# The last 64 keys of each head over 128 rows, and the causal masks at the end of their score banks

## The chip, the cores and the metric

The kernel runs on one core of a Trainium2 chip. What counts is the device time of one execution in microseconds, here the median of several runs. TensorE (PE) multiplies and writes PSUM banks. ScalarE (ACT), VectorE (DVE) and GpSimd (POOL) work on PSUM and SBUF. SyncE (SP) issues all DMAs of this kernel. PEld in the profile is TensorE's weight load, which can run beside a matmul.

## The reference

Attention over 4 x 8 heads with 576 positions of width 64, then two feed-forward blocks over the 2304 resulting rows. Cut to what matters:

```python
scores = scale * np.matmul(q, k.transpose(0, 1, 3, 2))
causal = np.triu(np.ones((S, S), dtype=bool), k=1)
cum = np.cumsum(np.maximum(s, 0.0), axis=-1)
bias = -(cum[:, :, :, None] - cum[:, :, None, :])
scores = np.where(causal, -1000000000.0, scores + np.minimum(bias, 0.0))
attn = softmax(scores)                     # max subtracted, sum + 1e-9
x = np.matmul(attn, v)                     # 32 heads, 576 x 64 each
h = x @ moe_w_in;   x = (h - np.tanh(h)) @ moe_w_out        # 512 -> 2048 -> 512
h = x @ moe2_w_in;  g = h * np.clip(h + 3, 0, 6) / 6;  out = g @ moe2_w_out
```

## The kernel before

**Stages.** PE first works through the 32 heads (until 208 us), then through the first feed-forward block (lines 831 and 862, until about 599 us), then through the second one, done with seven products instead of eight (lines 1123 and 1199, to the end). ACT, DVE and POOL prepare operands beside it, and in the attention they also turn the feed-forward weights, which come as 64-bit numbers, into pairs of high and low 32-bit parts (lines 753 to 780).

**A head.** Scores are computed transposed: keys on the 128 PSUM partitions, queries along the free dimension. 576 keys are four tiles of 128 and one tile of 64 (`j` = 4). For each head:

- Line 481 (`mx`) multiplies queries with keys for the row maxima; line 490 on DVE (`rd`, tile `junk`) reduces them into `Mt`; lines 515 to 519 bring them into the layout `mrow`, and two DMAs write them out and into the rows of `Q1` (`mdram<-mrow`, `Q<-mdram`).
- Line 575 (`st`) fills four score banks, 0 to 3. `CHUNKS` says which tile of keys `j` and which queries lie in a bank; `STEPS` gives the order of its matmuls. A step `h` multiplies the tiles `K2` and `Q2` over 128 rows, a step `l` the tiles `K1` and `Q1` over 68 rows (two of them carry the cumulative sum, two the maximum), and the number behind the letter is the place in `CHUNKS`. The step `m` adds the causal mask: it multiplies the bf16 identity `identb` with columns of `maskT`, 128, 192 or 256 of them (banks 0, 2 and 3; bank 1 has none). The first step of a bank carries `start`, the last one `stop`.
- Line 578 on ACT (`ex`) takes the exponential of a bank into a tile `pt`.
- Line 606 (`pv`) multiplies V (`vf`, 66 columns: 64 of V, then ones for the row sums) with `pt` and sums into two banks. These operands are 32-bit floats in full precision, and the trace has two matmul records for each such multiplication, two passes. In bank 2 the first product belongs to the last 64 keys (`j` = 4): 64 rows, 64 columns.
- Line 629 on ACT (`ov`) copies the sums out, and line 636 stores the row of sums.

**What sets the order.** All instructions of all engines stand in an order that a planner works out ahead (`Plan.schedule`, with the priorities of `PRIO` and costs by the number of columns). Neither costs nor priorities depend on the order of `STEPS` or on the number of rows, so that the order around the change stays. In PE's order the four banks of one head's scores stand between the sums (line 606) and the maxima (line 481) of its neighbours.

**Tables that the change touches.** The values of V arrive as 640 rows, of which the last 64 are zeros (`values` in `_layout`). In bank 2 the 64 keys fill partitions 0 to 63 of the first 64 columns; on partitions 64 to 127 of these columns only the mask is written, and it is -8e9 there, so that `pt` is 0.

Of the kernel before, what the change touches and what calls it, by code (L numbers as in the profile page):

```python
# [19 lines left out]
B, H, S, D = 4, 8, 576, 64  # L20
NT, DM, DFF = B * S, H * D, 2048
P = 128
# [3 lines left out]
DV = D + 2  # L26
# [18 lines left out]

MASKS = [(1, 64, 128), None, (1, 0, 192), (2, 64, 128)]

STEPS = ["h0 m l0", "h0 l0", "h1 h0 l0 m l1", "h1 h0 m l1 l0"]

MAXT = [[(2, 384, 0), (4, 576, 384)], [(3, 512, 0)], [(1, 256, 0), (0, 128, 256)]]  # L50
TINY, HUGE = (float(np.array([b], np.uint32).view(np.float32)[0]) for b in (0x38000000, 0x47F00000))
# [177 lines left out]
def mm_us(n, f32=False):  # L229

    return (4 * n / 2.4 + 6) / 1e3 if f32 else max(0.1, (n / 2.4 + (13 if n > 128 else 5)) / 1e3)


def vec_us(n, ghz, fixed):
    return (n / ghz + fixed) / 1e3
# [3 lines left out]
def kernel(  # L239
# [55 lines left out]
    def r(b):  # L295
        return late[b.t] if isinstance(b.t, str) else b.t
# [260 lines left out]
    def scores(h, hh, t0, b1, b2, vf, deps, lv, xp, xb, bt, sds):  # L557
        def st(c, b):
            qa, ka, qb, kb = (t[:, hh] for t in r(b1) + r(b2))
            ps = r(b)  # L560
            segs = CHUNKS[c]

            def step(x):
                if x == "m":
                    k, m0, n = MASKS[c]
                    o = ps[:, 0 : k * 192].rearrange("p (k n) -> p k n", k=k)[:, :, 0:n]
                    return o, identb, maskT[:, m0 : m0 + k * n].rearrange("p (k n) -> p k n", k=k)
                kk, qq, n_r = (kb, qb, P) if x[0] == "h" else (ka, qa, 68)
                j, q0, n, col = segs[int(x[1])]
                rr = min(P, S - j * P)  # L570
                return ps[0:rr, col : col + n], kk[0:n_r, j * P : j * P + rr], qq[0:n_r, q0 : q0 + n]

            mms = [step(x) for x in STEPS[c].split()]
            for i, (o, w, x) in enumerate(mms):
                nc.tensor.matmul(o, w, x, start=(i == 0), stop=(i == len(mms) - 1), skip_group_check=True)  # L575

        def ex(c, b, pt):
            nc.scalar.activation(r(pt), r(b)[:, 0 : CW[c]], AF.Exp, scale=0.125)  # L578

        exs, pts, sts = [], [], []  # L580
        for c in range(4):
            b, pt = Buf(banks), Buf(ptp[c])
            us = sum(2 * mm_us(n) for _, _, n, _ in CHUNKS[c]) + (mm_us(MASKS[c][0] * MASKS[c][2]) if MASKS[c] else 0)
            so = plan.op("PE", us, lambda c=c, b=b: st(c, b), deps, [b1, b2, b], t0 + PRIO["st"] + PRIO["dst"] * c, name=f"st{h}_{c}")
            sts.append(so)
            exs.append(plan.op("ACT", vec_us(CW[c], 1.2, 165), lambda c=c, b=b, pt=pt: ex(c, b, pt), [so], [b, pt], t0 + PRIO["ex"] + PRIO["dst"] * c, name=f"ex{h}_{c}"))
            pts.append(pt)
        st_done[h] = sts
        po = [Buf(banks, greedy=True) for _ in range(2)]

        def segments(c):
            segs = []
            for j, q0, n, col in CHUNKS[c]:
                if q0 < 256:
                    n0 = min(256 - q0, n)
                    segs.append((j, 0, q0, n0, col))
                    if n > n0:
                        segs.append((j, 1, 0, n - n0, col + n0))
                else:
                    segs.append((j, 1, q0 - 256, n, col))  # L600
            return segs

        def pv(c):
            for j, bank, oc, n, col in segments(c):
                rr = min(P, S - j * P)
                nc.tensor.matmul(  # L606
                    r(po[bank])[0:DV, oc : oc + n], r(vf)[0:rr, j, hh, :], r(pts[c])[0:rr, col : col + n],
                    start=(j == 0), stop=(bank == 0 and c == 2) or (bank == 1 and j == 2),
                )

        pvs = []
        for c in range(4):
            us = sum(mm_us(n, True) for _, _, _, n, _ in segments(c))
            used = sorted({x[1] for x in segments(c)})
            pvs.append(plan.op(
                "PE", us, lambda c=c: pv(c), [exs[c], lv] + pvs[-1:],
                [vf, pts[c]] + [po[i] for i in used], t0 + PRIO["pv"] + PRIO["dst"] * c, name=f"pv{h}_{c}",
            ))
        pv_done.extend(pvs)

        sg = Buf(stagep) if hh else None
        own = [sg] if hh else [xb]

        def ov(bank):
            q0, n = ((0, 256), (256, 320))[bank]
            dst = r(sg) if hh else xp()
            nc.scalar.activation(dst[0:DV, q0 : q0 + n], r(po[bank])[0:DV, 0:n], AF.Copy)

        ov0 = plan.op("ACT", 0.36, lambda: ov(0), [pvs[2]], [po[0]] + own, t0 + PRIO["ov"], name=f"ov{h}_0")
        ov1 = plan.op("ACT", 0.42, lambda: ov(1), [pvs[3], ov0], [po[1]] + own, t0 + PRIO["ov"], name=f"ov{h}_1")

        def sd_():
            src = r(sg) if hh else xp()
            nc.sync.dma_start(sdram[bt, h % H : h % H + 1, :], src[D : D + 1, :])

        sd = plan.dma(sd_, 2, [ov1], own, t0 + PRIO["sd"], name=f"sd{h}")
        batch_sd.setdefault(bt, []).append(sd)
        if hh:  # L640
            so = plan.dma(lambda: nc.sync.dma_start(xp()[64:128], r(sg)[0:D, :]), 147, [sds[0], ov1], own + [xb], t0 + PRIO["so"], name=f"so{h}")
            batch_so.setdefault(bt, []).append(so)
        return sd
# [678 lines left out]
```

## Time and profile before

| what | value |
|---|---|
| median of 3 runs | 967.13 us (966.61 to 970.09) |
| the profiled execution | 967.26 us, of which the span of its instructions 965.5 us |
| PE busy | 943.3 us, 98% of the span |
| DVE, ACT, POOL busy | 671.8, 467.6, 160.8 us |
| granted clock of PE | 1.00 |

The profile's page gives for each engine how long it was busy, and the chain of work that ended last: from the last instruction back to whatever released each one. The windows view gives busy time by stretch; the timeline gives the instructions in order of time, with runs of the same line merged to one row. A matmul's start in the trace is when it enters the engine, and its end is modelled, so that neighbours overlap; distances from one start to a later start are what can be added up.

### The profile page before, as it was taken

What the parts mean: (1) busy time and instruction counts of PE and PEld (TensorE: products, weight loads), DVE (VectorE), ACT (ScalarE), POOL (GpSimd) and SP (SyncE); (2) the same over time, 40 slices, a digit from 0 to 9 for tenths busy, and PEclk for the clock granted to TensorE, in tenths of its full rate; (3) what the DMA queues carried; (4) which work ended last, traced back from release to release, by engine and by line L of the source; (5) the groups of instructions that cost most, each with busy time, mean ns of one, the idle gap of its engine ahead of it and who ended that gap; (6) DMA issues with size and microseconds to landing.
All of it is one profiled execution on the core that took longest, in us unless ns stands there. A gap on an engine that the chain in (4) does not pass through costs nothing.

```text
span 965.5 us, 14956 instructions
## 1 busy us (share of the span) xinstructions
PE 943.3 (98%) x5560; PEld 833.1 (86%) x5560; DVE 671.8 (70%) x1107; ACT 467.6 (48%) x714; POOL 160.8 (17%) x106
## 2 busy tenths in 40 slices
PE   3999999999999999999999999999999999999998
PEld 3777777778878888998888888999999999999998
DVE  7887767769998667767766834556775567764763
ACT  2677677755444443543443433444454434544442
POOL 8344656520000000003223222000000000000000
PEclk9999999999999999999999999999999999999999
DMA  4767777677535357556455690776797767977663
GB/s 123 183 165 177 212 189 202 161 253 255 172 115 189 141 209 239 174 183 224 158 214 170 221 319 30 249 218 211 237 321 229 226 208 238 319 223 228 207 220 104
DMA packets 70521, 195.91 MB, mean 203 GB/s; under 512 B 11634, under 2 KB 20338, under 8 KB 69168
## 3 DMA queue, kind: packets, MB, share of 16 engines
q1 hardware_dynamic: 70448, 194.95, 63.5%
q8 instruction: 44, 0.72, 0.3%
q14 instruction: 29, 0.24, 0.1%
HBM read 143.75 MB, written 44.09 MB: 195 GB/s over the span
## 4 chain that ended last, share of the span: by engine, by line
PE 93%; DVE 3%; DMA 2%; ACT 1%; issue 1%; SPq 0%; DVEq 0%; ACTq 0%
PE bank L831 20%; PE bank L862 20%; PE pair L1199 19%; PE pair L1123 18%; PE bank L606 9%; PE bank L575 5%; PE wide L481 1%; DVE junk L490 1%; PE bank L481 1%; DMA Q<-Q 1%; DMA Q<-mdram 0%; ACT w L779 0%; DVE K L430 0%; DVE f_w L1143 0%; DMA K<-rb 0%
## 5 line engine op out<-in xcount | busy, mean ns | idle before, releaser
L862 PE MATMUL bank<-gg,w 128*128 128x512 f32 (+1 forms) x960 | 234.3, 368 | 0.5 <-ACT gg L850 0.3
L831 PE MATMUL bank<-xx,w 128*128 128x512 f32 (+1 forms) x960 | 233.3, 368 | 0.0
L862 PEld LDWEIGHTS bank<-gg,w 128*128 128x128 f32 x960 | 170.1, 189 | 30.9 <-ACT gg L850 1.3
L831 PEld LDWEIGHTS bank<-xx,w 128*128 128x128 f32 x960 | 170.5, 188 | 30.3
L1123 PE MATMUL pair<-op_w,w 128*128 128x384 f32 x648 | 118.0, 334 | 0.6 <-DVE f_w L1143 0.6
L842 ACT ACTIVATE g<-bank 128x512 f32<-128x512 f32 (+1 forms) x80 | 44.5, 556 | 147.6 <-PE bank L831 124.3
L1199 PE MATMUL pair<-w,op_W 128*128 128x256 f32 x918 | 115.1, 283 | 0.0
L1123 PEld LDWEIGHTS pair<-op_w,w 128*128 128x128 f32 x648 | 112.4, 188 | 1.2 <-DVE f_w L1143 0.9
L1199 PEld LDWEIGHTS pair<-w,op_W 128*128 128x128 f32 x918 | 112.8, 192 | 0.0
L606 PE MATMUL bank<-pt,vf 128*66 128x320 f32 (+4 forms) x448 | 112.3, 364 | 0.3 <-ACT pt L578 0.3
L852 POOL TENSOR_TENSOR gg<-g,gg 128x512 fp32r<-128x512 f32 x32 | 47.5, 1485 | 345.0 <-ACT gg L850 307.9
L575 PE MATMUL bank<-Q,K 128*128 128x320 f32 (+9 forms) x384 | 98.0, 368 | 1.6 <-DMA Q<-mdram 1.2
L846 DVE TENSOR_TENSOR g<-bank,g 128x512 f32<-128x512 f32 (+1 forms) x80 | 50.9, 636 | 64.8 <-ACT g L842 64.1
L578 ACT ACTIVATE pt<-bank 128x512 f32<-128x512 f32 (+2 forms) x128 | 63.1, 501 | 40.9 <-PE bank L575 36.4
L575 PEld LDWEIGHTS bank<-Q,K 128*128 128x128 f32 (+3 forms) x384 | 64.8, 188 | 20.7 <-DMA Q<-mdram 1.3
L850 ACT ACTIVATE gg<-g 128x512 fp32r<-128x512 f32 (+1 forms) x80 | 47.0, 587 | 43.3 <-DVE g L846 35.0
L606 PEld LDWEIGHTS bank<-pt,vf 128*66 128x66 f32 (+1 forms) x448 | 52.3, 138 | 14.4 <-issue 1.9
L490 DVE CUSTOM_DVE_ANT_0 junk<-bank,maskA 128x512 bf16<-128x512 f32 (+2 forms) x96 | 45.0, 469 | 27.0 <-PE bank L481 19.6
L427 POOL TENSOR_TENSOR Q<-tq,Q 64x1152 fp32r<-64x1152 f32 (+1 forms) x17 | 42.4, 2494 | 57.7 <-DMA tq<-in_k_dram 13.0
L490 DVE CUSTOM_DVE_ANT_0 junk<-wide,maskA 128x384 bf16<-128x384 f32 x64 | 41.8, 653 | 9.2 <-PE wide L481 4.6
L437 POOL TENSOR_TENSOR K<-tq,K 64x1152 fp32r<-64x1152 f32 (+1 forms) x17 | 42.8, 2520 | 23.7 <-DVE K L430 7.4
L1199 PE MATMUL pair<-w,op_B 128*128 128x256 f32 x342 | 44.1, 283 | 0.0
(305 smaller groups left out, 1299.3 us busy)
## 6 DMA issues: line engine op xcount, KB each, us to landing
w<-wdram SPq DMA_DIRECT2D x149, 512.0 KB
wdram<-cv SPq DMA_DIRECT2D x56, 512.0 KB
raw_c<-in_w_dram SPq DMA_DIRECT2D x11, 1024.0 KB
raw_b<-in_w_dram SPq DMA_DIRECT2D x11, 1024.0 KB
raw_a<-in_w_dram SPq DMA_DIRECT2D x12, 512.0 KB
vf<-in_v_dram SPq DMA_DIRECT2D x16, 330.0 KB
rb<-rdram SPq DMA_DIRECT2D x8, 576.0 KB
xdram<-xb SPq DMA_DIRECT2D x16, 288.0 KB
```

Source lines behind the costliest of these rows:

```text
L490: nc.vector.tensor_tensor_reduce(out=junk[0:rr, 0:w], in0=r(b)[0:rr, col : col + w], in1=maskA[0:rr, m0 : m0 + w], scale=1.0, scalar=-3.0e ...
L575: nc.tensor.matmul(o, w, x, start=(i == 0), stop=(i == len(mms) - 1), skip_group_check=True)
L578: nc.scalar.activation(r(pt), r(b)[:, 0 : CW[c]], AF.Exp, scale=0.125)
L606: nc.tensor.matmul(r(po[bank])[0:DV, oc : oc + n], r(vf)[0:rr, j, hh, :], r(pts[c])[0:rr, col : col + n], start=(j == 0), stop=(bank == 0 ...
L831: nc.tensor.matmul(r(ps)[:, 0:w], wt[:, c, :], x(c)[:, 0:w], start=(part == 0 and c == 0), stop=(part == 2 and c == NCC - 1),)
L842: nc.scalar.activation(r(g)[:, 0:w], r(ps)[:, 0:w], AF.Tanh)
L846: nc.vector.tensor_sub(x, r(ps)[:, 0:w], x)
L850: gho = plan.op("ACT", vec_us(w, 1.2, 205), lambda: nc.scalar.activation(r(gh)[:, 0:w], r(g)[:, 0:w], AF.Copy), [m, to_gg], [g, gh], base)
L852: glo = plan.op("DVE" if beside else "POOL", vec_us(w, 0.96, 155) if beside else vec_us(w, 0.44, 160), lambda: (nc.vector if beside else n ...
L862: nc.tensor.matmul(r(acc[e])[:, 0:w], a[:, es], bb[:, 0:w], start=f, stop=l)
L1123: nc.tensor.matmul(bank(k)[:, l], w[hw][:, l, kc], r(x)[:, hx, kc], start=(i in (1, 5, 2) and j == 0 and kc == 0), stop=(j == 2 and kc == ...
L1199: nc.tensor.matmul(r(c[k])[:, m * 256 : (m + 1) * 256], r(x)[:, hx, l, m * P : (m + 1) * P], w[hw][:, l], start=(i == order[chain_first[k] ...
```

## The change

The order of the steps in three of the four score banks, and the rows of one product with V:

```diff
-STEPS = ["h0 m l0", "h0 l0", "h1 h0 l0 m l1", "h1 h0 m l1 l0"]
+STEPS = ["h0 l0 m", "h0 l0", "h1 l1 h0 l0 m", "h1 h0 l1 l0 m"]
...
         def pv(c):
             for j, bank, oc, n, col in segments(c):
-                rr = min(P, S - j * P)
                 nc.tensor.matmul(
-                    r(po[bank])[0:DV, oc : oc + n], r(vf)[0:rr, j, hh, :], r(pts[c])[0:rr, col : col + n],
+                    r(po[bank])[0:DV, oc : oc + n], r(vf)[:, j, hh, :], r(pts[c])[:, col : col + n],
                     start=(j == 0), stop=(bank == 0 and c == 2) or (bank == 1 and j == 2),
                 )
```

`rr` was 64 for `j` = 4 and 128 for all other tiles. That is 1 product of 7 in each of the 32 heads. On ACT, DVE, POOL and SP the order of the instructions and the semaphores that they wait for are the same in both programs; on PE only steps within a bank change places.

PE's order before, around a bank 0 (`bank3_71`), the first products of another head with V, and a bank 2 (`bank1_66`); `Q2`, `K2` are the tiles of the `h` steps, `Q1`, `K1` those of the `l` steps, and the last column is the output's shape:

```order
L606 MATMUL bank5_73<-pt1_0_113,vf0_108 66x320
L575 MATMUL bank3_71<-Q2_1_106,K2_1_107 128x256
L575 LDWEIGHTS identb_128
L575 MATMUL bank3_71<-maskT_127,identb_128 128x128
L575 MATMUL bank3_71<-Q1_3_102,K1_3_103 128x256
L606 MATMUL bank5_73<-pt2_0_115,vf0_108 66x64
L606 MATMUL bank0_65<-pt2_0_115,vf0_108 66x128
```

The same place in the changed program:

```order
L605 MATMUL bank5_73<-pt1_0_113,vf0_108 66x320
L575 MATMUL bank3_71<-Q2_1_106,K2_1_107 128x256
L575 MATMUL bank3_71<-Q1_3_102,K1_3_103 128x256
L575 LDWEIGHTS identb_128
L575 MATMUL bank3_71<-maskT_127,identb_128 128x128
L605 MATMUL bank5_73<-pt2_0_115,vf0_108 66x64
L605 MATMUL bank0_65<-pt2_0_115,vf0_108 66x128
```

The mask's weight load and matmul moved behind the `l` step, so that the product with V (66x64, now over 128 rows) follows a mask and no longer an `l` step. In bank 2 of the same head, before:

```order
L575 MATMUL bank1_66<-Q2_1_106,K2_1_107 128x448
L575 MATMUL bank1_66<-Q2_1_106,K2_1_107 64x64
L575 MATMUL bank1_66<-Q1_3_102,K1_3_103 64x64
L575 LDWEIGHTS identb_128
L575 MATMUL bank1_66<-maskT_127,identb_128 128x192
L575 MATMUL bank1_66<-Q1_3_102,K1_3_103 128x448
L606 MATMUL bank5_73<-pt3_0_117,vf0_108 66x192
```

and in the changed program:

```order
L575 MATMUL bank1_66<-Q2_1_106,K2_1_107 128x448
L575 MATMUL bank1_66<-Q1_3_102,K1_3_103 128x448
L575 MATMUL bank1_66<-Q2_1_106,K2_1_107 64x64
L575 MATMUL bank1_66<-Q1_3_102,K1_3_103 64x64
L575 LDWEIGHTS identb_128
L575 MATMUL bank1_66<-maskT_127,identb_128 128x192
L605 MATMUL bank5_73<-pt3_0_117,vf0_108 66x192
```

Here too the mask is last, and the next product with V follows it. By the same lists, a mask of bank 0 is followed by a product with V in 28 of 32 heads (22 of them the one of the 64 keys), one of bank 2 in 17, one of bank 3 in 8; the other 43 masks are followed by a matmul of line 575 or 481.

## Rows read from the trace of the kernel before

**Rows 1.** The page: PE's busy time and instructions, and the last chain.
```profile
PE 943.3 (98%) x5560; PEld 833.1 (86%) x5560; DVE 671.8 (70%) x1107; ACT 467.6 (48%) x714; POOL 160.8 (17%) x106
PE 93%; DVE 3%; DMA 2%; ACT 1%; issue 1%; SPq 0%; DVEq 0%; ACTq 0%
```
**Rows 2.** Windows: busy us (instructions) by engine, then clock, DMA share, GB/s.
```profile
39.20:47.80 8.60, 8.22 (x52) 5.99 (x50) 7.52 (x28) 5.11 (x11) 3.29 (x2) 1.00 0.92 210
47.80:185.70 137.90, 137.90 (x840) 103.69 (x839) 105.27 (x332) 99.60 (x184) 74.89 (x33) 1.00 0.68 181
185.70:196.00 10.30, 9.93 (x57) 6.79 (x56) 5.55 (x7) 8.45 (x17) 6.85 (x4) 1.00 0.89 205
196.00:208.00 12.00, 12.00 (x69) 8.52 (x70) 8.87 (x16) 7.28 (x16) 3.73 (x3) 1.00 0.75 244
```
**Rows 3.** Waits: who waited for whom, us in total, times, longest.
```profile
PE bank L575 <- DMA Q<-mdram: 1.2, 1, 1.2
PE bank L575 <- DMA Q<-Q: 0.4, 1, 0.4
...
DVE junk L490 <- PE bank L481: 19.6, 18, 2.6
```
**Rows 4.** PE's timeline, one head in the steady stretch: start, us, instruction.
```profile
65.72 0.70 PE L606 MATMUL bank<-pt,vf 128*66 128x320 f32 x2
66.02 0.52 PE L575 MATMUL bank<-Q,K 128*128 128x256 f32 x1
66.38 0.23 PE L575 MATMUL bank<-maskT,identb 128*128 128x128 bf16 x1
66.42 0.36 PE L575 MATMUL bank<-Q,K 68*128 68x256 f32 x1
66.71 1.23 PE L606 MATMUL bank<-pt,vf 64*66 64x64 f32 x6
67.54 1.00 PE L575 MATMUL bank<-Q,K 128*128 128x320 f32 x5
68.38 0.26 PE L575 MATMUL bank<-maskT,identb 128*128 128x192 bf16 x1
68.42 0.45 PE L575 MATMUL bank<-Q,K 68*128 68x448 f32 x1
68.71 1.03 PE L606 MATMUL bank<-pt,vf 128*66 128x192 f32 x4
69.34 0.64 PE L575 MATMUL bank<-Q,K 128*128 128x320 f32 x2
```
**Rows 5.** PE's timeline, a bank 0 that is followed by a product over 128 rows.
```profile
200.54 0.23 PE L575 MATMUL bank<-maskT,identb 128*128 128x128 bf16 x1
200.58 0.37 PE L575 MATMUL bank<-Q,K 68*128 68x256 f32 x1
200.78 0.70 PE L606 MATMUL bank<-pt,vf 128*66 128x320 f32 x2
```
**Rows 6.** Weight loads' timeline (PEld), around the same head as rows 4.
```profile
66.38 0.10 PEld L575 LDWEIGHTS <-identb 128*128 128x128 bf16 x1 [0.20 <-issue]
66.38 0.20 PEld L575 LDWEIGHTS bank<-Q,K 68*128 68x128 f32 x1
66.71 0.13 PEld L606 LDWEIGHTS bank<-pt,vf 64*66 64x66 f32 x1
```
**Rows 7.** Groups by shape: 34 to 39.2, 47.8 to 185.7, 185.7 to 196, 196 to 208 us.
```profile
L606 PE MATMUL bank<-pt,vf 64*66 64x64 f32 x2 | 0.3, 244 | 0.0
...
L606 PE MATMUL bank<-pt,vf 64*66 64x64 f32 x48 | 7.9, 244 | 0.0
...
L606 PE MATMUL bank<-pt,vf 64*66 64x64 f32 x4 | 0.7, 244 | 0.0
...
L606 PE MATMUL bank<-pt,vf 64*66 64x64 f32 x6 | 1.0, 244 | 0.0
```
**Rows 8.** The last chain in order of time: start, us, what.
```profile
39.26 0.56 DVE junk L490
39.85 0.75 DVE junk L490
40.67 0.70 PE wide L481 x3
...
43.22 0.61 ACT pt L578
...
185.73 10.13 DMA Q<-Q
...
196.00 0.60 PE bank L575 x3
...
660.76 2.15 PE pair L1199 x18
```
**Rows 9.** DVE's timeline at the end of the attention.
```profile
207.33 2.49 DVE L818 TENSOR_TENSOR xx<-xr,xx 128x512 fp32r<-128x512 f32 x4
213.27 0.69 DVE L846 TENSOR_TENSOR g<-bank,g 128x512 f32<-128x512 f32 x1 [3.45 <-ACT g L842]
```
**Rows 10.** POOL's and PE's timelines: last operand of a pair of heads, its first scores.
```profile
110.23 2.62 POOL L437 TENSOR_TENSOR K<-tq,K 64x1152 fp32r<-64x1152 f32 x1 [0.85 <-DVE K L430]
...
117.74 0.52 PE L575 MATMUL bank<-Q,K 128*128 128x256 f32 x1
```

## The prediction

> **What bounds the kernel now.** I read the page first: PE is busy for 98% of the span, and 93% of the chain that ended last runs over PE [rows 1]. The change lies in the attention alone, which ends at 208 us, so the second view is the windows of that stage. From 47.8 to 185.7 us, and again from 196 to 208 us, PE has no idle time at all, at a granted clock of 1.00, while DVE, ACT and POOL have a quarter or more of idle time [rows 2]. The third view says who waits: PE hardly waits for anyone, while DVE waits 19.6 us for PE's maxima [rows 3]. So the attention's length is PE's own, and what PE saves there is saved, except in two stretches. At the start, from 39.2 to 47.8 us, the chain goes back and forth between DVE's row maxima, ACT's exponentials and PE [rows 8], and PE idles for 0.4 us [rows 2]. And from 185.7 to 196 us the chain is a transfer of 10.13 us, `Q<-Q`, for the last pair of heads [rows 8], for which PE waits 0.4 us [rows 3]. In both, PE's savings turn into more waiting.
>
> The fourth view is PE's timeline over one head [rows 4]. Since ends are modelled, I compare starts.
>
> **The change part by part: 128 rows instead of 64.** Take bank 0 and the sums that follow it. From the mask's start to the start of the 64-row product it is 66.71 - 66.38 = 0.33 us [rows 4]; from the mask's start to a product over 128 rows, with the same two score steps between, it is 200.78 - 200.54 = 0.24 us [rows 5]. So entering the 64-row product costs 0.09 us. The weight loads show it: those of the 64-row product start only with it, at 66.71, and not during the step before [rows 6].
>
> Then the group itself. Its six passes (two of 64 columns, two of 128, two of 320) start at 66.71, and the next scores start at 67.54: 0.83 us [rows 4]. What should they take? A pair of 320-column passes puts its follower 66.02 - 65.72 = 0.30 us later, and the follower starts some 0.03 us after the last pass, so that a pass is 0.27 us, or 0.84 ns a column; the four passes at 68.71 agree (2 x 0.16 + 0.27 + 0.03 = 0.62 us against 69.34 - 68.71 = 0.63) [rows 4]. At that price the six are 2 x 0.055 + 2 x 0.11 + 0.27 + 0.03 = 0.63 us. The other 0.20 us are the way back: the loads of the first pass of either kind lie open, and the array stands between them.
>
> Both together are 0.29 us a head. With 128 rows the product stands as any other among its neighbours; its own columns, weights (66 columns) and records stay, so I take the whole 0.29 us as removed. As a lower bound, a 64-column pass could fail to hide its own weight load. I have no row of a 64-column pass over 128 rows in two passes; the nearest is the 128-column one in the same group.
>
> How many heads count? All 32 have the product, in two passes each; 24 lie between 47.8 and 185.7 us, three behind 196 us and one between 34 and 39.2 us [rows 7]. Of the other four, two lie before or in the DVE-bound start and two in the 10 us of the transfer [rows 7], and these I count at nothing: DVE's maxima and the `Q<-Q` transfer hide them. That gives 28 x 0.29 = 8.1 us.
>
> **The masks.** A mask's weight load never runs ahead: `identb` is loaded only when the mask starts, after PEld had nothing to do for 0.20 us, and the step behind it starts 0.04 us later [rows 4, 6]. That load stays open wherever the mask stands. The load behind a mask, of 128 columns for a score step, starts with the mask [rows 6] but is longer than a mask of 128 columns. Score steps of 256 columns stream at 2.15 / 18 = 0.12 us each in the second block [rows 8], and a mask of 128 at half of that. Bank 0 before: 0.24 us for mask and `l0` [rows 5]. After: 0.12 for `l0`, whose load now hides behind `h0`, then 0.04 + 0.06 for the mask, 0.22 us, if the load of V's 66 columns behind it is hidden. That saves 0.02 us at the 28 banks 0 that a product with V follows, 0.6 us in all and 0.5 us in the heads that count. For bank 2 the same sum comes out even (its mask is 192 columns long), and for bank 3 the mask already covers the next load; both I take as nothing. The 43 masks before a matmul of line 575 or 481 keep the transition that rows 6 show today, only with another partner.
>
> What no row shows is a mask followed by a product with V: 53 places. It goes from bf16 to a two-pass f32 product. From below: hidden, as the score step's load is, and then also cheaper by some hundredths. From above: as the entry to the 64-row product with its open load. I take the hidden load, since the row nearest in kind is the load that starts 0.00 us after the mask [rows 6].
>
> **What is late next.** Exponentials come when the mask, not `l`, ends; the bank as a whole is not longer. A faster head asks POOL and DVE for operands sooner. POOL ends the last operand of a pair at 112.85 us, and PE wants it at 117.74 us [rows 10]: 4.9 us of slack, against 0.6 us that a pair gets shorter. At the end DVE works without a break until 209.8 us on the inputs of the first feed-forward block [rows 9], which does not move with the last two heads' gain; I take off 0.3 us for that, half of their 0.6. Behind it DVE waits 3.45 us for ACT and PE [rows 9], so that the rest passes on into the block.
>
> Sum: 8.1 + 0.5 - 0.3 = 8.3 us. The profiled execution took 967.26 us, 0.1 us from the median; 967.26 - 8.3 gives 958.9 us.
>
> **The rivals.**
>
> *The mask drains PE as the 64 rows did.* If a change from bf16 to V's product costs what entering the 64 rows cost (0.09 us and an open load of some 0.055), 53 places x 0.145 x 28/32 = 6.7 us come back, and bank 0's 0.5 us go: 8.1 - 0.3 - 6.7 = 1.1 us gained, 966.2 us. For it speaks that `identb`'s own load does not run ahead; against it that the load behind a mask does. Chance 0.10.
>
> *Loads of the same rows do not overlap.* Within the group, loads of 128-row products start while the pass before them still streams, since four passes at 68.71 us take no more than their columns [rows 4]. By this the two passes of 64 columns hide their loads too; were each load open, they would cost 2 x 0.055 us more, 28 x 0.18 = 5.0 us would be left of 8.1, and the time would be 967.26 - 5.0 - 0.5 + 0.3 = 962.1 us. Chance 0.05. The Trainium skill, "TensorE: Matmul & The Clock Gate", Part 3, The mechanism, states the rule behind this: weight loads overlap matmuls in flight only where the row groups differ. It speaks against giving all products the same rows, and the trace contradicts it for V's products over 128 rows.
>
> *Another engine takes over.* In the steady stretch DVE is busy for 105 of 138 us and POOL for 75 [rows 2], and the program makes some of POOL's work wait its turn behind DVE's. If the faster pace runs into that halfway, half of the 8.3 us is left: 963.1 us. Against it speaks DVE's 19.6 us of waiting for PE [rows 3]. Chance 0.12.
>
> *The change does not do what it says*: the cost comes with the 64 columns and not with the 64 rows. Then only the masks' 0.5 us is left, 966.8 us. Against it: the 0.09 us lie before the product and cannot hang on its columns. Chance 0.03.
>
> *Slower: the bf16 mask before V's product costs as much as the whole visit to 64 rows and back.* That is 0.29 us at 53 places, 28/32 of it 13.4 us, against 7.8 saved: 972.9 us. It decides from 7.8 / 46 = 0.17 us a place. Masks are followed by f32 steps today at 0.04 us, with no such price [rows 4]. Chance 0.06.
>
> **How the numbers follow.** The forecast, 958.9 us, has 0.64. The measurement can tell about 0.5%, 4.8 us, from no change: faster is below 962.3 us. That holds the forecast, the rival of the loads at its edge and half of the one of the engines, 0.75; slower is the last rival, 0.06; the rest, 0.19, is within 0.5%. The range reaches down to all 32 heads at 0.29 us with 1.4 us for the masks, 967.3 - 10.7, with a little below it for a mask that V's product makes cheaper still: 956.0. Up, it takes in the loads and the engines: 964.5. Outside are the drain, the columns and slower, 0.19.
>
> **What would show it.** In the changed profile the record of the 64-column product should read 128*66. From the start of its group to the next scores it should be 0.63 us and not 0.83. From the mask of bank 0 to the product behind it, it should be 0.10 us; 0.15 to 0.25 us would be the drain. The attention should end near 199.5 us, with PE still without idle time up to the `Q<-Q` wait, which should grow from 0.4 to about 1 us. It is wrong if PE idles between 40 and 180 us, or if line 606's group stays at 0.8 us.

## The result, and the profile after

The changed kernel took 960.34 us (median of 6 runs, 957.06 to 961.55) beside 967.46 us of the kernel before on the same chip (6 runs, 966.37 to 970.09): a ratio of 0.9919, 95% interval 0.9897 to 0.9940, some 7 us or 0.8% faster. Two repetitions gave 960.23 us (0.9930, 0.9914 to 0.9946) and 958.52 us (0.9918, 0.9905 to 0.9932). The forecast was 958.9 us. One thing must be kept in mind for all that follows: the changed kernel's times lie over 4 us and more, and the execution that was profiled first is the shortest of its six, 957.06 us (span 955.3 us).

The page after, PE's busy time and the shares of the last chain, as in [rows 1]:

```profile
PE 933.0 (98%) x5560; PEld 831.9 (87%) x5560; DVE 672.8 (70%) x1107; ACT 464.9 (49%) x714; POOL 161.2 (17%) x106
PE 92%; DVE 3%; DMA 2%; ACT 1%; issue 1%; SPq 0%; DVEq 0%; ACTq 0%
```

PE is busy for 10.3 us less; ACT is busy for 2.7 us less, and the other engines differ by 1.2 us at most. The windows after, with stretches moved to the same places of the program as in [rows 2] (columns as there), and below them one of PE's waits, as in [rows 3]:

```profile
47.80:178.00 130.20, 129.07 (x836) 101.83 (x835) 104.17 (x332) 96.36 (x183) 73.86 (x33) 1.00 0.73 193
178.00:186.20 8.20, 8.20 (x54) 6.44 (x53) 5.06 (x6) 7.26 (x15) 5.91 (x3) 1.00 0.95 225
```

```profile
PE bank L575 <- ACT stage L628: 1.1, 1, 1.1
```

Two things differ from what stood there before. In the long stretch PE now idles for 130.20 - 129.07 = 1.1 us, all of it in one wait of line 575 for an ACT copy (line 628, `ov`; from line 606 on, line numbers are one less in the changed kernel). And the wait for `Q<-Q` is gone from the list.

One head of PE's timeline after, to be laid beside [rows 4]: start, us, instruction.

```profile
64.28 0.64 PE L575 MATMUL bank<-Q,K 128*128 128x256 f32 x2
64.76 0.23 PE L575 MATMUL bank<-maskT,identb 128*128 128x128 bf16 x1
64.83 1.04 PE L605 MATMUL bank<-pt,vf 128*66 128x64 f32 x6
65.47 1.20 PE L575 MATMUL bank<-Q,K 128*128 128x320 f32 x6
66.51 0.26 PE L575 MATMUL bank<-maskT,identb 128*128 128x192 bf16 x1
66.61 1.03 PE L605 MATMUL bank<-pt,vf 128*66 128x192 f32 x4
67.23 0.90 PE L575 MATMUL bank<-Q,K 128*128 128x320 f32 x4
```

The product of the last 64 keys reads 128*66. Between starts, before and after: bank 0 to V's product 66.71 - 66.02 = 0.69 and 64.83 - 64.28 = 0.55 us; the group of six passes 0.83 and 0.64 us; bank 2 to the next product with V 68.71 - 67.54 = 1.17 and 66.61 - 65.47 = 1.14 us; its four passes 0.63 and 0.62 us. That is 0.36 to 0.37 us a head. The weight loads of the same stretch (PEld), beside [rows 6]:

```profile
64.76 0.10 PEld L575 LDWEIGHTS <-identb 128*128 128x128 bf16 x1
64.76 0.55 PEld L605 LDWEIGHTS bank<-pt,vf 128*66 128x66 f32 x6
```

V's loads begin at 64.76, 0.07 us before their product enters at 64.83; before, they began together with it, at 66.71 [rows 6].

Inside the group the single passes can be told apart in short windows, which leave out the passes that have ended. The rows below begin at the second, the third and the fourth pass. Before:

```profile
66.82 0.48 PE L606 MATMUL bank<-pt,vf 64*66 64x64 f32 x2
66.97 0.33 PE L606 MATMUL bank<-pt,vf 128*66 128x128 f32 x1
67.14 0.54 PE L606 MATMUL bank<-pt,vf 128*66 128x128 f32 x2
```

and after:

```profile
64.89 0.34 PE L605 MATMUL bank<-pt,vf 128*66 128x64 f32 x2
64.95 0.39 PE L605 MATMUL bank<-pt,vf 128*66 128x128 f32 x2
65.06 0.54 PE L605 MATMUL bank<-pt,vf 128*66 128x128 f32 x2
```

From the first pass to the second it is 0.11 us before and 0.06 after, from there to the first pass of 128 columns 0.15 and 0.06, and one pass further 0.17 and 0.11; behind that the distances are the same. So the way to 64 rows costs 0.09 us ahead of the group and 0.05 in it, and the way back to 128 rows 0.09 and some 0.05 us.

The attention ends 10.0 us earlier: the last chain has line 831 start behind the last products with V at 208.03 us before, and line 830 at 198.07 us after. The two profiled executions are 10.2 us apart (967.26 and 957.06 us), so that this gain passes whole through both feed-forward blocks.

### The profile page after: what moved, and what is told of

Same layout as the page of the kernel before. It is cut to its first block, busy times and chain, and to the rows that moved or that the text cites. A ratio compares the mean times of both kernels' runs of the same rounds, so it can differ in the third digit from the quotient of the medians.

```text
span 955.3 us, 14956 instructions
## 1 busy us (share of the span) xinstructions
PE 933.0 (98%) x5560; PEld 831.9 (87%) x5560; DVE 672.8 (70%) x1107; ACT 464.9 (49%) x714; POOL 161.2 (17%) x106
## 4 chain that ended last, share of the span: by engine, by line
PE 92%; DVE 3%; DMA 2%; ACT 1%; issue 1%; SPq 0%; DVEq 0%; ACTq 0%
PE bank L830 20%; PE bank L861 20%; PE pair L1198 19%; PE pair L1122 18%; PE bank L605 8%; PE bank L575 5%; DVE junk L490 1%; PE wide L481 1%; DMA tq<-in_q_dram 1%; PE bank L481 1%; DMA Q<-mdram 0%; DMA rdram<-rb 0%; ACT w L778 0%; DVE K L430 0%; DVE f_w L1142 0%
## 5 line engine op out<-in xcount | busy, mean ns | idle before, releaser
L605 PE MATMUL bank<-pt,vf 128*66 128x320 f32 (+4 forms) x448 | 106.9, 360 | 0.3 <-ACT pt L578 0.3
L575 PE MATMUL bank<-Q,K 128*128 128x320 f32 (+9 forms) x384 | 88.7, 352 | 1.6 <-ACT stage L628 1.1
L605 PEld LDWEIGHTS bank<-pt,vf 128*66 128x66 f32 x448 | 50.5, 141 | 6.7 <-ACT pt L578 0.5
```

The source lines that it names most:

```text
L605: nc.tensor.matmul(r(po[bank])[0:DV, oc : oc + n], r(vf)[:, j, hh, :], r(pts[c])[:, col : col + n], start=(j == 0), stop=(bank == 0 and c ...
```

## The experiments

Each time stands beside runs of the kernel before on the same chip (medians 966.4 to 967.5 us). "Rows" is the product over 128 rows, "masks" the new order of the steps.

### The two edits apart

Rows alone, with the masks at their old places:

```diff
-                rr = min(P, S - j * P)
-  ... r(vf)[0:rr, j, hh, :], r(pts[c])[0:rr, col : col + n],
+  ... r(vf)[:, j, hh, :], r(pts[c])[:, col : col + n],
```

> The changed kernel with the masks back in their old places: the product of the last 64 keys runs over 128 rows, nothing else is new. Theory (the visit to 64 rows and back costs 0.28 to 0.29 us a head, and the masks' new places bring the rest of the 0.36 us a head that the changed kernel's trace shows): PE's time from a mask of bank 0 to the first product behind it stays 0.24 us, the group of six passes takes 0.63 us, and the attention is 30 x 0.28 = 8.4 us of PE's time shorter than before; 959 to 961 us. Rival (the masks carry most of it): 964 to 966 us.

Measured: 961.45 us (960.25 to 964.46), ratio 0.9944 (0.9931 to 0.9957), 5.75 us faster.

Masks alone, with 64 rows:

```diff
-STEPS = ["h0 m l0", "h0 l0", "h1 h0 l0 m l1", "h1 h0 m l1 l0"]
+STEPS = ["h0 l0 m", "h0 l0", "h1 l1 h0 l0 m", "h1 h0 l1 l0 m"]
```

> The kernel before with the masks last in their banks, the product of the last 64 keys over 64 rows as before. Theory: the drain before the 64 rows and the open loads stay, bank 0 gives about 0.03 us and bank 2 another 0.03 us a head, so that 1 to 2 us are gained: 965.5 to 966.5 us. Rival (the masks carry most of the gain): 958 to 961 us.

Measured: 965.53 us (964.42 to 966.48), ratio 0.9981 (0.9972 to 0.9989), 1.67 us faster. The changed kernel ran in the same comparison:

> The changed kernel once more, for another profile and more times. Its six runs lay between 957.1 and 961.6 us, and the profiled one was the fastest, with PE idle for 1.1 us near 140 us behind a load of queries that landed 9.0 us after its issue. Theory (what the slower runs lose is lost in waits for DMAs in the attention): a profile near 960 us shows 3 to 5 us of PE idle between 40 and 200 us where the fastest shows 1.1, and the same distances between PE's instructions elsewhere. Rival: the idle time is the same and PE's own pace differs, in the attention or behind it.

Measured: 960.23 us (958.35 to 964.45), 6.97 us faster. The profile fell on the shortest of these runs, 958.35 us, so that the 3 to 5 us of idle time that were expected near 960 us were not seen and the two theories stay undecided: between 40 and 200 us PE idles for 1.7 us here, and for 1.5 us in the profile of 957.06 us. The edits add up, 5.75 + 1.67 = 7.4 us, but they are less than the timeline of a head says: there the rows are worth 0.09 us on entry and 0.19 in the group, 0.28 us in each of up to 32 heads. In the chain of the rows alone there is a transfer that was not there before; the chain's pieces (start, us, what):

```profile
91.96 6.91 DMA K<-cdram
...
99.01 0.67 PE wide L481 x3
```

PE waits 1.1 us for it in the middle of the attention; in the list of before the one wait for `K<-cdram` lies at the start. That turned the question to the transfers.

### The changed kernel's new wait

In the changed kernel the new wait of 1.1 us stands at 140.98 us. Its chain, piece by piece:

```profile
129.03 0.62 SPq L664
...
130.42 9.01 DMA tq<-in_q_dram
...
139.45 0.05 ACT Q L421
...
140.52 0.42 ACT stage L628
...
140.98 0.57 PE bank L575 x3
```

Line 664 spreads the row sums of a batch's eight heads over the partitions, two transfers of 576 KB on SP's queue. Right behind them the same queue takes the queries of the next pair of heads, `tq<-in_q_dram`, and these take 9.01 us to land. ACT reaches line 421, which needs them, waits, and the copy of line 628 that stands behind it on ACT frees the bank that PE wants. Before, the same load was issued at 135.28 us and ACT's instruction ran at 144.26 us, 8.98 us later, without a wait for that load. The two rows are from SP's and from ACT's timeline of before (a wait would stand in brackets at the end):

```profile
135.28 0.57 SPq L442 DMA_DIRECT2D tq<-in_q_dram  x1
```

```profile
144.26 1.17 ACT L421 ACTIVATE Q<-tq 64x1152 fp32r<-64x1152 f32 x1
```

So the kernel before needed the load 8.98 us after its issue. When it landed there no row shows; where ACT waited for it in other kernels with the same spreading, it landed 8.7 to 9.4 us after its issue (rows alone 8.96, masks alone 9.40, the changed kernel once more 8.76). The kernel before had next to nothing to spare. Nor does the changed kernel lose the 1.1 us every time: its second profile (958.35 us) has the same wait, the third (956.78 us) has none, and ACT waits for 0.58 us there and not for 1.83.

To price the transfer, the next kernel spreads the sums of one quarter only. It leaves out the sums of six of a batch's eight heads, so that its output is not the reference's:

```diff
-   dst = r(rb)[i * D : (i + 1) * D].rearrange("p (c s) -> p c s", c=NCC)
-   nc.sync.dma_start(dst, src[i : i + 1].broadcast_to([D, NCC, S]))
+   dst = r(rb)[i * D : (i + 1) * D, 0:S].rearrange("p (c s) -> p c s", c=1)
+   nc.sync.dma_start(dst, src[i : i + 1, 0:1].broadcast_to([D, 1, S]))
...
-   ... tensor_mul(x, x, r(rb)[:, c * S : (c + 1) * S])
+   ... tensor_mul(x, x, r(rb)[:, 0:S])
```

> The changed kernel with a quarter of the broadcast of the row sums: only the sums of the first two heads of a batch are spread and used for all eight, 295 KB instead of 1180 KB in each of four batches, all instructions in the same order. Theory (the load of queries near 130 us and its like wait behind this broadcast in the DMA queues): the wait near 140 us is gone, the median comes to 956 to 957.5 us, and the runs lie closer together than 4.5 us. Rival (the broadcast has no part in it): 958 to 961.5 us, as the changed kernel.

Measured: 956.52 us, and its four runs lie within 955.98 to 957.08 us; ratio 0.9889 (0.9875 to 0.9903). The window that had 1.1 us of idle time has none:

```profile
47.80:178.00 130.20, 130.20 (x843) 103.13 (x843) 104.03 (x333) 97.37 (x184) 75.84 (x33) 1.00 0.67 180
```

That alone could also be a gain that any kernel has from a smaller transfer. So the same cut, with the same sums left out, was made in the kernel before, and in the kernels with one edit each:

> The kernel before, with the row sums of one quarter of a batch's rows spread instead of all four (288 KB instead of 1152 KB per batch through SP's queue; the sums of six of eight heads of a batch are left out, so the output is not the reference's). Theory (only the faster kernel reaches the queue's delay): before has no wait there, so its time stays, 966.5 to 967.3 us, and the whole 3.7 us between the changed kernel with and without the full spreading belong to the changed kernel's own waits. Rival (the smaller transfer helps any kernel): 3 to 4 us faster, 963.5 us, and then the changed kernel loses nothing by it.

Measured: 966.58 us (966.26 to 967.27), ratio 0.9994 (0.9985 to 1.0003). The kernel before gains 0.4 us, which is no more than its noise.

> The 128 rows alone with the masks at their old places, and the quarter of the spreading (sums of six of eight heads left out). If the queue's delay took part of what the rows alone gave (5.75 us timed; 7.6 us in the trace without PE's waits), now 959.2 to 959.8 us; the forecast's own term was 28 x 0.29 = 8.1 us, 959.0. Rival (the rows are worth the timed 5.75 us and nothing was lost): 961.4 us, less whatever the kernel before gains from the same cut.

Measured: 957.95 us (957.80 to 958.67), ratio 0.9908 (0.9894 to 0.9922), over 1 us below the range that was expected.

> The masks last with 64 rows, and the quarter of the spreading (sums of six of eight heads left out). Masks alone gave 1.67 us. If the two edits add up without the queue's delay, rows 7.7 and masks 1.7 us make 9.4, and 1.3 us of the 10.7 us of both together must come from having both (the mask next to V's product of 128 rows): then this run is 965.5 us. If the masks were worth more and lost it in the queue: 964 to 964.5 us.

Measured: 964.54 us (964.28 to 965.54), ratio 0.9973 (0.9963 to 0.9982).

Without the long transfer, then, the rows are worth 966.58 - 957.95 = 8.6 us, the masks 966.58 - 964.54 = 2.0 us, and both 966.58 - 956.52 = 10.1 us. With it they are worth 5.75, 1.67 and 7.0 to 8 us. That the edits are worth only what was first timed falls with this, and so does a gain that any kernel has from the cut. The transfer takes 2 to 3 us from the rows and from both edits, and nearly nothing from the masks alone, which leave the kernel only 1.7 us faster.

Two kept traces show where it is lost. With the rows alone, the 64-column product with V starts at 86.87, 92.67 and 99.51 us in three successive heads, and with the rows and the short transfer (a quarter of the spreading) at 87.08, 92.54 and 98.02 us: 0.3 and 1.4 us are lost right behind the first spreading (issued at 89.57 us), which is the wait for `K<-cdram` above. Another 0.5 us is lost behind the second one (from 137.77 to 143.26 us, against 136.27 to 141.30), and 0.8 us at the transfer `Q<-Q` behind the third (from 186.20 to 190.64, against 184.35 to 188.03). Together these are 2.9 us, and the two profiled executions are 960.59 - 957.94 = 2.65 us apart. So the long transfer costs time in three places of the attention.

The same starts price the edits by the head. Among the four kernels with the short transfer, the 16 distances that lie between 49 and 141 us in the kernel before are shorter by 0.28 us on average with the rows, by 0.08 us with the masks and by 0.36 us with both.

These kernels also show each term by itself. With 128 rows and old masks, bank 0 and what follows:

```profile
64.62 0.52 PE L575 MATMUL bank<-Q,K 128*128 128x256 f32 x1
64.98 0.23 PE L575 MATMUL bank<-maskT,identb 128*128 128x128 bf16 x1
65.02 0.36 PE L575 MATMUL bank<-Q,K 68*128 68x256 f32 x1
65.22 1.04 PE L605 MATMUL bank<-pt,vf 128*66 128x64 f32 x6
65.86 0.98 PE L575 MATMUL bank<-Q,K 128*128 128x320 f32 x5
```

From the mask to the product it is 0.24 us, to the hundredth what [rows 5] had promised against 0.33 in [rows 4], and the group takes 0.64 us. With masks last and 64 rows:

```profile
66.20 0.23 PE L575 MATMUL bank<-maskT,identb 128*128 128x128 bf16 x1
66.36 1.23 PE L606 MATMUL bank<-pt,vf 64*66 64x64 f32 x6
67.18 1.20 PE L575 MATMUL bank<-Q,K 128*128 128x320 f32 x6
```

Here 0.16 us lie between mask and product, 0.09 more than with 128 rows (64.83 - 64.76 = 0.07), and the group takes 0.82 us. Whatever stands ahead of it, a visit to 64 rows costs 0.09 us on entry and 0.18 to 0.20 us in the group.

It is not any smaller number of rows that costs. The `l` steps run over 68 rows among products over 128; in the changed kernel an `l` step of 256 columns enters behind an `h` step, and the mask, over 128 rows again, follows 0.12 us later:

```profile
64.64 0.28 PE L575 MATMUL bank<-Q,K 68*128 68x256 f32 x1
64.76 0.23 PE L575 MATMUL bank<-maskT,identb 128*128 128x128 bf16 x1
```

That is what 256 columns take among products that are all over 128 rows (2.15 / 18 = 0.12 us, [rows 8]). The way in is as cheap: an `h` step of 192 columns has its `l` step 0.09 us behind it in the same trace. What between 64 and 68 rows makes the difference was not tried.

### Is it the rows, or the narrow passes?

If the visit costs, a second one must cost as much again. The product of the 64 keys was cut into two of 32 columns, one first and one last among the sums, both over 64 rows; and, as its control, the same cut was made in the changed kernel, over 128 rows:

```diff
+            segs = segments(c)
+            if c == 2:
+                j, bank, oc, n, col = segs[0]
+                segs = [(j, bank, oc, n // 2, col)] + segs[1:] + [(j, bank, oc + n // 2, n // 2, col + n // 2)]
-            for j, bank, oc, n, col in segments(c):
+            for j, bank, oc, n, col in segs:
```

> The kernel before, with the product of the 64 keys cut in two of 32 columns, one first and one last among the sums of bank 2, both over 64 rows: a second visit to 64 rows in each head. Theory (a visit costs 0.29 us, 0.09 on entry and 0.20 in the group, though here the way back is taken by the next scores): 28 x 0.25 to 0.29 = 7 to 8 us slower, 974 to 975 us. Rival (the cost goes with the narrow passes and not with the rows): two passes more, of 32 columns all four, cost what they cost over 128 rows too, 1 to 3 us, 968 to 970 us.

Measured: 979.13 us (978.63 to 979.57), ratio 1.0122 (1.0100 to 1.0144), 12.05 us slower: more than either had expected.

> The changed kernel with the same cut: two products of 32 columns, first and last among the sums of bank 2, both over 128 rows. Two more passes whose weight loads do not hide behind 32 columns: 28 x 0.04 to 0.12 = 1 to 3.4 us slower than the changed kernel, 961 to 964 us. If it grows as much as the kernel before grows by the cut (7 to 8 us, 967 to 968 us), the cost is that of narrow passes and not of the 64 rows.

Measured: 961.40 us (960.95 to 962.82), ratio 0.9940 (0.9920 to 0.9960): 1 to 3 us above the changed kernel, and 4.9 us above 956.5 us, which the changed kernel takes without the long transfer. Since this one runs slower than that, the second is the fairer comparison; PE's list of waits shows no ACT copy here, but 0.6 us for `Q<-Q`.

PE's timelines, first with two visits to 64 rows, then with the same passes over 128 rows (the first row runs over all eight passes of the group, whose shapes differ):

```profile
68.56 1.44 PE L610 MATMUL bank<-pt,vf 64*66 64x32 f32 x8
69.93 0.85 PE L575 MATMUL bank<-Q,K 128*128 128x320 f32 x5
...
70.95 1.03 PE L610 MATMUL bank<-pt,vf 128*66 128x192 f32 x4
```

```profile
65.71 1.13 PE L609 MATMUL bank<-pt,vf 128*66 128x32 f32 x8
66.68 1.04 PE L575 MATMUL bank<-Q,K 128*128 128x320 f32 x6
67.56 0.26 PE L575 MATMUL bank<-maskT,identb 128*128 128x192 bf16 x1
67.66 0.33 PE L609 MATMUL bank<-pt,vf 128*66 128x192 f32 x1
```

With 64 rows the group grows from 0.83 to 1.37 us and the scores behind it shrink from 1.17 to 1.02 us, 0.39 us in all. With 128 rows the group grows from 0.64 to 0.97 us and the scores shrink from 1.14 to 0.98 us, 0.17 us in all. The likely reason why the scores shrink, not tested, is that a long last pass used to stream on beside their first record. The narrow passes thus cost 0.17 us over 128 rows, which the expectation had put at 0.04 to 0.12. If they cost as much over 64, the second visit costs 0.39 - 0.17 = 0.22 us more. In times: 12.05 - 4.9 = 7.2 us, or 0.22 us in 32 heads. The rival, that the cost comes with narrow passes, explains a part of what this cut costs but not the difference between 64 and 128 rows.

### A version that keeps the gain

The spreading can be made in four pairs of transfers, one for each quarter, so that other loads can be issued between them. All sums are spread:

```diff
-        sp = plan.dma(spread, 1180, [wr, co], [rb], t0 + 7, name=f"sp{bt}", n=2)
+        sp = [plan.dma(lambda c=c: spread(c), 295, [wr, co], [rb], t0 + 7 + 0.01 * c,
+                       name=f"sp{bt}_{c}", n=2) for c in range(NCC)]
...
-   no = plan.op(..., norm, [sp, batch_so[bt][c]], ...)
+   no = plan.op(..., norm, [sp[c], batch_so[bt][c]], ...)
```

> The changed kernel, with the spreading of a batch's row sums done as four pairs of transfers of 288 KB in all, one for each quarter, rather than one pair for all; nothing is left out. If the delay comes from the length of one pair in the queue ahead of the next heads' loads, which can now go in between, 956.5 to 958 us and a narrow spread of the runs. If it is the sum of the bytes, or the quarters leave together: 960 us as the changed kernel, with its spread of 4 us. If eight issues on SP in place of two hold up the other DMAs: 961 to 963 us.

Measured: 956.98 us (956.52 to 958.68), ratio 0.9901 (0.9886 to 0.9917). Then the changed kernel and this one side by side:

> The changed kernel once more, beside the one with the spreading in four pairs: 960.2 us, as the two times before, with runs from 957 to 964 us.

Measured: 958.52 us (956.78 to 960.55), ratio 0.9918 (0.9905 to 0.9932).

> The changed kernel with the spreading of row sums in four pairs of transfers, on the same chip as the changed kernel itself. If the shorter pairs free the queue for the next heads' loads: 956.5 to 957.5 us again, some 3 us below the changed kernel, and a narrower spread. If the 957.0 us measured was chance or the chip: the same time as the changed kernel within 1 us.

Measured: 956.55 us (956.09 to 957.23), ratio 0.9897 (0.9882 to 0.9912). That is 2.0 us below the changed kernel, where 3 had been expected, and the two ratios' intervals overlap. Over all runs it is 956.7 us (8 runs, 956.09 to 958.68) against 959.9 us (17 runs, 956.78 to 964.45). The spread is what changes most: the best of the changed kernel's executions are as short as these, and of the long ones, over 959 us, there is none among the eight. SP's timeline of the first run of this kernel, and from ACT's timeline the instruction that waited:

```profile
128.16 1.19 SPq L664 DMA_DIRECT2D rb<-rdram  x2
129.44 0.55 SPq L442 DMA_DIRECT2D tq<-in_q_dram  x1
...
130.67 1.23 SPq L664 DMA_DIRECT2D rb<-rdram  x2
```

```profile
135.19 1.17 ACT L421 ACTIVATE Q<-tq 64x1152 fp32r<-64x1152 f32 x1 [1.35 <-DMA tq<-in_q_dram]
```

The queries now stand behind a quarter of the spreading, and land 135.19 - 129.44 = 5.75 us after their issue, not 9.01. The Trainium skill ("DMA: Bandwidth & Descriptors", Queues, rings and completion order) says that an engine takes a ring's descriptors in their order; the two numbers agree. The planner gave ACT another order here too, so that the shorter landing is not the only thing that changed. It is not free of waits (the list of waits of the same run):

```profile
PE bank L861 <- ACT gg L849: 1.7, 2, 1.3
```

In the first feed-forward block PE now waits 1.3 us for ACT at one place, which the changed kernel does not (0.3 us there). Why was not tried; another 1 us may lie there.

## Why the prediction was right, and where it was not

**The bound.** Right. PE's own length set the attention, and what PE saved reached the end: 10.0 us at 198.07 us and 10.2 us between the profiled executions.

**The row term**, 0.09 us on entry and 0.20 us in the group. Right to 0.02 us: 0.28 us a head by the starts of many heads, entry 0.09 us (0.24 against 0.33, and 0.07 against 0.16), group 0.64 us against the 0.63 that was computed from the price of a column, and 8.6 us in time against 8.1 forecast. Only the place of the 0.20 us was not quite right: it is not all the way back, since 0.05 us of it lie between the two passes over 64 rows. The passes of 64 columns over 128 rows hide their weight loads: 0.64 us leave no room for two open loads of 0.055 us. That also answers the rival of the loads of the same rows: the rule in the Trainium skill ("TensorE: Matmul & The Clock Gate", Part 3, The mechanism), that loads overlap only where the row groups differ, does not hold for this kernel's products. The same section also lets a load run ahead into a background weight buffer; no run here tells whether these loads go there.

**The heads that count.** Half of this step failed: it left out four heads, and two of them counted. Between the kernels with the short transfer (the one before and the one with both edits), every distance between heads from 49 us on but one (0.20 us) shrinks by 0.32 to 0.38 us, those of the two heads beside the `Q<-Q` transfer too (0.35 and 0.32); the one in the stretch bound by DVE's maxima, from 41 to 49 us, shrinks by 0.08 us, as had been said. So some 30 heads counted rather than 28: 8.6 us at 0.28 us a head are 31. The two heads beside the `Q<-Q` transfer were taken as hidden by its 10.13 us [rows 8], and its wait was to grow from 0.4 to 1 us. It vanished in the profiled execution (with the rows alone it is 0.5 us). What I had missed is that the transfer's issue rides on PE's pace itself: it left SP at 185.73 us before and 177.81 us after, 7.9 us earlier. A long transfer in the chain is a fixed length, not a fixed point in time.

**The masks.** The forecast was 0.5 us, and the runs say 2.0 us. The mis-sized term is the mask with its own load in bank 0. I added 0.04 us for the load and 0.06 for the streaming; the mask's start is 0.07 us ahead of V's product (64.76 and 64.83), so that bank 0 gives 0.05 us a head (65.22 - 64.62 = 0.60 in the kernel with rows alone, 0.55 after) rather than 0.02. Bank 2, counted at nothing, gives 0.01 to 0.03 us (1.14 us against 1.15 with rows alone and 1.17 before). That is 0.06 to 0.08 us a head, and the starts of many heads gave 0.08. The unseen transition from a bf16 mask to V's product went the way that was taken as likeliest: 0.07 us, below the 0.10 expected; 0.15 to 0.25 us would have been the drain, so that both rivals of a mask that drains PE fall.

**The end.** The 0.3 us taken off for DVE's inputs did not show: the gain is 10.0 us at the attention's end and 10.2 us at the kernel's.

**What was left out.** These terms make 10.1 us rather than 8.3, and the time would have been 957 us. The kernel took 958.5 to 960.3 us because SP's queue took 2 to 3 us back. It is the rival "another engine takes over", with a chance of 0.12, but not by the engine it named: PE's lists of waits name neither DVE nor POOL in the attention from 30 us on, and a transfer had no slack. The prediction had looked at POOL's 4.9 us of slack [rows 10] for the operands and had not looked at when the load in front of them lands. The sign of the forecast was right by its mechanism, but that 958.9 us came so close was in part luck, since two errors went against each other, about 1.8 us too little gain on PE, and about 2 to 3 us of loss not seen.

**What stays open.** Each of the three profiles of the changed kernel caught the shortest execution of its comparison (957.06, 958.35 and 956.78 us). The one of 958.35 us loses a little behind the first spreading too: two heads take 5.80 and 5.69 us there, and their neighbours 5.38 to 5.40. Where the executions of 960 us and more lose their time follows from the trace of the rows alone and from the cut, which takes the spread away; no trace shows one of them. Nor is the granted clock ruled out for the very longest: it was 0.997 or 0.998 on average in five executions of 961.28 to 964.46 us (three of the changed kernel, two with the rows alone), and 0.999 or 1.00 in the others; without those the changed kernel's times still reach from 956.8 to 961.6 us. Nor do the runs say which of the cut's effects does it, fewer bytes in all or a shorter block ahead of the queries; the version with four pairs moves all bytes and speaks for the second.

## What to carry to other kernels

On TensorE a lone product over fewer rows than its neighbours can cost more than the zeros that would fill it up: here 64 rows among 128 cost 0.28 us a visit (68 rows cost nothing that a row shows), which a few starts in the timeline show before anything is changed. Ahead of a faster inner loop, list not only which engines have slack, but for each load how long it takes from issue to landing and how long after its issue it is needed; 8.98 us from issue to need in the kernel before, and 9.01 us to land in the changed one, is a bound that no list of waits had shown. And a broadcast that is not urgent can be cut into pieces: the queries behind a quarter of it landed 5.75 us after their issue, behind all of it 9.01.

## What the runs showed of the hardware

- The price of changing from 128 rows to 64 and back appears on both sides: 0.09 us ahead of the product and 0.05 at its second pass, and 0.09 and some 0.05 us on the way back, with the same columns and the same number of passes. A second visit in the same head cost 0.22 us. Between 128 and 68 rows no such price shows.
- Two passes more of 32 columns cost 0.17 us a head over 128 rows, although the columns are the same in all; what part of it is weight loads that 32 columns don't cover was not taken apart.
- A bf16 matmul of 128 columns is followed by a two-pass f32 product 0.07 us later; the change of type cost nothing that a row shows.
- The same load of 288 KB landed 9.01 us after its issue behind two transfers of 576 KB, and within 5.75 us behind two of 144 KB.
